# One row-half group per four token tiles in place of two, in a kernel of linear attention beside a gated feed-forward layer

## The chip, the cores and the metric

The kernel runs on one core of a Trainium2 chip. The metric is the device time of one execution in microseconds (us). The engines are PE (matrix products; its weight loads are listed as PEld), DVE (vector), ACT (scalar functions), POOL (a second vector-like engine) and SP, which here only issues transfers. They run side by side, each through its own queue in order, and wait for one another by semaphores.

## The reference

For 2048 tokens of 640 features the output is `g * a + (1 - g) * b`, with a gate `g = sigmoid(sum(x * gate_w))` per token. Branch `b` is a feed-forward layer:

```python
g = silu(x @ w_gate)          # 640 -> 1728
u = x @ w_up                  # 640 -> 1728
b = (g * u) @ w_down          # 1728 -> 640
```

Branch `a` is linear attention over 32 heads of 20 features:

```python
phi_q = concat(softmax(q @ w_phi), softmax(-(q @ w_phi)))   # 40 features per head
phi_k = concat(softmax(k @ w_phi), softmax(-(k @ w_phi)))
kv  = einsum("bhsf,bhsd->bhfd", phi_k, v)
num = einsum("bhqf,bhfd->bhqd", phi_q, kv)
a   = (num / (phi_q . sum(phi_k) + 1e-6)) @ wo
```

Two facts matter here. The hidden width 1728 is 13 x 128 + 64: the last chunk of the contraction in `(g * u) @ w_down` has only 64 rows. And the products with `w_down` and with `wo` go into the same sums, since the gate has been folded in before.

## The kernel before

The tokens are cut into 16 tiles of 128 (`NT`) and four blocks of four tiles (`NB`). The program is written out as a list of items in the string `ORDER`; each item is a letter with numbers, and the dictionary `ops` at the end maps the letter to a function. The items are emitted in this order, and every engine's queue gets its instructions in it. A tracker (`_Tracker`) adds the semaphore waits from the buffers that an instruction reads and writes. So `ORDER` alone sets which instruction stands behind which on each engine.

Up to the item N the list projects keys and values (U, V, K), builds the combined matrices (M, R), normalizes the keys (S on DVE, P on POOL) and sums `kv` (E). From there on the items are:

- `Q t` (`qtile`): the query projection of tile t on PE (ten matmuls of 320 columns), two exponentials on ACT into one of three `eq` buffers.
- `A t`, `B t`, `C t`: DVE's part of the normalization: a reduction (A), a product with the row `zb` (B), and a second reduction with five small instructions (C: `qw`, `qm`, `qd`, its reciprocal, `qc`).
- `c t` (`qmul`): POOL scales `eq` into `ph`, and SP transposes `ph` into `phiT` by a transfer.
- `F b.k` (`fitem`): chunk k of the hidden layer for block b. PE makes the gate and the up projection (five matmuls of 512 columns each) in the two banks of a PSUM pair, ACT a tanh into `hT` and a copy of the up part into one of three `us` buffers, DVE a product that reads the gate bank (line 332), POOL the product of both (line 328). `F b.13` is the last chunk, of 64 rows: it is laid out so that tiles 0 and 2 of a block lie in the rows 0 to 63 of `hT[.., 13, ..]` and tiles 1 and 3 in the rows 64 to 127, and `wd[:, 13, :]` holds the last 64 rows of `w_down` in both halves.
- `O b.part` (`oitem`): the attention output of block b in three parts, copied by ACT to `oT` and `ol`; `o b` (`omove`): SP moves `ol` into `oT` by four transfers.
- `W b.p` (`hitem`): the half-row products. For tiles 2p and 2p+1 of the block it takes a PSUM pair each and opens their sums with the 64-row chunk. The matmuls of the two tiles alternate, and since they use different halves of the rows of the array, two of them can run at once.
- `D b.u` (`ditem`): the output of tile u: 13 full chunks of `hT` and five of `oT`, each in two column parts of 320, so 36 matmuls, which go on with the sums that W opened; then ACT scales the sums by the gate (`omg`) into `osb` and SP stores them. The last tile (15) is done in three parts, of 320, 224 and 96 columns, so that the last store is small.
- `Z` transposes the denominators, from which `zb` is loaded; `J` (`gates`) makes the gate values on DVE and ACT; `L` loads the late weights.

PSUM has eight banks, used as four pairs. `next_pair` gives the pair that was used least recently and is not in `held`; W puts the pairs that it opens into `held` and D takes them out. An item that takes a pair waits for all that still reads it. `mm` emits a list of matmuls as one unit: the waits of all its operands stand ahead of its first matmul, and one semaphore is raised at its last. All matmuls have the line 300 (in `mm`), all activations the line 318.

The functions that the change touches are `hitem`, `ditem` and `parts`, the fills (`fills(3)`) and `ORDER`.

Of the kernel before, what the change touches and what calls it, by code (L numbers as in the profile page):

```python
# [1 line left out]

# [1 line left out]

# [4 lines left out]
P = 128  # L9
S_TOK = 2048  # L10
D = 640
# [3 lines left out]
NT = S_TOK // P  # L15
NB = 4
# [8 lines left out]
ACTF = mybir.ActivationFunctionType  # L25
# [3 lines left out]
BF16 = DT.bfloat16  # L29
# [12 lines left out]
U0.3 U1.3 U2.3 U0.4 U1.4 U2.4 V3 Y F0.1 M1 i3 M0 F0.0 M2 V4 M3 M4 K0 K1 I S0 V6 V5 S1 P0 K3 K2 P1 E0  # L42
V9 K4 E1 S3 V7 P3 K5 S2 V8 V10 S4 P2 P4 E2 R0 E3 K6 S5 P5 S6 i4 E4 V14 K7 K8 P6 V15 S7 R2 E5 K9 S8
P7 R1 E6 K10 S9 V12 P8 E7 P9 K11 S10 P10 F0.2 R3 F1.2 E8 E9 K12 E10 S11 S12 K14 S14 V11 K13 P11 P12
E11 K15 P14 R4 S13 P13 F1.9 S15 P15 E12 V13 T F1.8 E13 F1.11 E14 Q1 E15 Q0 Q2 N Z A1 A0 J A2 F0.7
F0.9 F1.4 B0 F1.12 B1 F0.4 L C0 F1.7 c0 F1.10 C1 F0.5 B2 c1 F0.11 Q3 C2 F1.0 F0.8 c2 F0.10 B3 Q4
F1.6 A3 C3 Q5 c3 F1.3 F0.13 F0.12 A4 F0.3 B4 F1.5 F0.6 O0.2 O0.1 O0.0 o0 C4 F1.1 F1.13 B5 A5 C5 Q6
c4 Q7 c5 Q8 W0.0 B7 A6 B6 C6 A7 c6 D0.1 D0.0 Q9 C7 W0.1 B8 A8 D0.2 C8 c7 Q10 D0.3 F2.10 F2.9 F2.2 c8
O1.2 A9 O1.1 B9 O1.0 B10 F2.8 o1 C9 Q11 c9 F2.5 F2.11 F2.4 Q12 B11 F2.3 A10 C10 B12 F2.7 A11 C11
W1.1 D1.3 D1.2 A12 c11 c10 Q14 W1.0 D1.0 A14 C12 D1.1 Q13 F3.2 F3.3 c12 O2.2 O2.1 B13 B14 O2.0 o2  # L50
F2.13 A13 F3.12 F3.5 F2.1 C14 Q15 F3.4 F3.9 F2.12 C13 F2.0 A15 c13 F2.6 c14 B15 F3.1 F3.0 F3.6 C15
c15 F3.13 W2.0 F3.7 D2.1 D2.0 F3.11 O3.2 O3.0 O3.1 F3.8 o3 F3.10 W2.1 D2.3 W3.0 D3.0 D3.1 D2.2 W3.1
D3.2 D3.3
"""


# [143 lines left out]
def _build(nc, A_x, A_wqkv, A_w_phi, A_wo, B_x, B_w_gate, B_w_up, B_w_down, gate_w, out):  # L200
    tr = _Tracker(nc)
    pe, act, dve, pool, sp = nc.tensor, nc.scalar, nc.vector, nc.gpsimd, nc.sync
# [3 lines left out]
    def sb(name, shape, dtype):  # L206
        t = nc.alloc_sbuf_tensor(name, list(shape), dtype)
        tr.reg(t, "sbuf", nc.lookup_mloc(t).addr)
        return t
# [5 lines left out]
    wd = sb("wd", [P, 14, D], BF16)  # L215
# [5 lines left out]
    osb = sb("osb", [P, 4, D], BF16)  # L221
# [10 lines left out]
    omg = sb("omg", [P, NT], F32)  # L232
# [9 lines left out]
    qd = sb("qd", [P, 2, 32], F32)  # L242
    qc = sb("qc", [P, 2, 66], F32)
    hT = sb("hT", [P, 2, 14, 512], BF16)

    wdbase = nc.lookup_mloc(wd).addr
    v1x = nc.alloc_sbuf_tensor_at("v1x", [P, NT - NV, 33 * 21], BF16, offset=wdbase)
# [32 lines left out]
    def bank(b, c0, c1, r0=0, r1=P):  # L280
        return ps[r0:r1, b * 512 + c0:b * 512 + c1]

    def halves(pr, n=320):

        return ps[:, pr * 1024:(pr + 1) * 1024].rearrange("p (b c) -> p b c", b=2)[:, :, 0:n]
# [5 lines left out]
    def mm(pairs):  # L291
        reads, writes = [], []
        for p in pairs:
            reads += [p[1], p[2]]
            writes.append(p[0])

        def fn():
            last = None
            for o, l, r, st, sp_, sk in pairs:
                last = pe.matmul(o, lhsT=l, rhs=r, start=st, stop=sp_, skip_group_check=sk)  # L300
            return last
        return run("pe", fn, list({id(a): a for a in reads}.values()), writes)

    def group(o, lr):
        n = len(lr)
        return [(o, l, r, i == 0, i == n - 1, False) for i, (l, r) in enumerate(lr)]
# [9 lines left out]
    def actop(o, i, func, scale=1.0):  # L316
        rd = [i] + ([scale] if isinstance(scale, bass.AP) else [])
        return run("act", lambda: act.activation(o, i, func, scale=scale), rd, [o])  # L318

    def copy(e, o, i):  # L320
        if e == "act":
            return actop(o, i, ACTF.Copy)
        eo = tr.eng[e]
        return run(e, lambda: eo.tensor_copy(o, i), [i], [o])
# [19 lines left out]
    def memset(e, a, v):  # L344
        eo = tr.eng[e]
        return run(e, lambda: eo.memset(a, v), [], [a])

    def dma(e, dst, src, transpose=False):
        eo = tr.eng[e]

        def fn():
            if transpose:
                return eo.dma_start_transpose(dst, src)
            return eo.dma_start(dst, src)  # L354
        rd = [src] if src.tensor.name in tr.base else []
        wr = [dst] if dst.tensor.name in tr.base else []
        return run(e, fn, rd, wr, dma=True)

    def select(ap, pattern, op, fill, base, cm):
        return run("pool", lambda: pool.affine_select(  # L360
            out=ap, in_=ap, pattern=pattern, compare_op=op, fill=fill, base=base,
            channel_multiplier=cm), [ap], [ap])
# [5 lines left out]
    out2 = out[0]  # L368
# [45 lines left out]
    def fills(i):  # L414
        if i < 2:
            v1v = (v1r, v1x)[i][:, :, :].rearrange("p b (h d) -> p b h d", d=DH + 1)
            memset("pool", v1v[:, :, H, :], 0.0)
            memset("pool", v1v[:, :, :, DH:DH + 1], 1.0)
        elif i == 2:
            memset("pool", ekr[:, :, 1280:FK], 0.0)  # L420
            memset("pool", krec[:, :, :], 0.0)
        elif i == 3:
            memset("pool", kvsb[:, :, :], 0.0)
            memset("pool", eq[:, :, 1280:FP], 0.0)
            memset("pool", qc[:, :, :], 0.0)
            memset("pool", hmask[:, :], 1.0)
            select(hmask[:, :], [[-40, 3]], ALU.is_ge, 0.0, 0, 1)
            select(hmask[:, :], [[40, 3]], ALU.is_gt, 0.0, 40, -1)
        else:
            memset("pool", ph[:, :, :], 0.0)  # L430
            memset("pool", zh[:, NCH:P], 0.0)

    for i in range(3):
        fills(i)
# [19 lines left out]
    held = set()  # L454

    def used(r):
        ring["lru"].remove(r)
        ring["lru"].append(r)
        return r

    def next_pair():
        return used([r for r in ring["lru"] if r < ring["n"] and r not in held][0])
# [268 lines left out]
    out_evs = []  # L731

    def stores_done():
        for n, v in out_evs[-4:-2]:
            sp.wait_ge(tr.sem[n], v)

    dpr = {}

    def parts(t):

        pr = dpr[t]
        if t < NT - 1:
            return [(2 * pr[0], 0, 320), (2 * pr[0] + 1, 320, D)]
        return [(2 * pr[0], 0, 320), (2 * pr[0] + 1, 320, 544), (2 * pr[1], 544, D)]

    def hitem(bt, p):

        todo = []
        for b in range(2):
            t = 4 * bt + 2 * p + b  # L750
            dpr[t] = [next_pair() for _ in range(1 + (t == NT - 1))]
            held.update(dpr[t])
            r = slice(64 * b, 64 * b + 64)
            todo.append([(bank(k, 0, c1 - c0), hT[r, bt % 2, 13, P * p:P * p + P], wd[r, 13, c0:c1], True, False, False)
                         for k, c0, c1 in parts(t)])
        mm([m for ab in zip_longest(*todo) for m in ab if m])

    def ditem(bt, u):
        buf = bt % 2
        t = 4 * bt + u  # L760
        tok = slice(P * u, P * u + P)
        ls = [(hT[:, buf, k, tok], wd[:, k, :]) for k in range(13)]
        ls += [(oT[:, buf, m, tok], wog[:, m, :]) for m in range(5)]
        n = len(ls)
        cols = [[(bank(k, 0, c1 - c0), l, r[:, c0:c1], False, i == n - 1, False) for i, (l, r) in enumerate(ls)]
                for k, c0, c1 in parts(t)]
        held.difference_update(used(r) for r in dpr[t])
        o = osb[:, t % 4, :]
        if t < NT - 1:
            mm([p for ab in zip(*cols) for p in ab])  # L770
            actop(o.rearrange("p (b c) -> p b c", b=2), halves(dpr[t][0]), ACTF.Copy, omg[:, t:t + 1])
            stores_done()
            out_evs.append(dma("sp", out2[t * P:(t + 1) * P, :], o))
            return
        for (b, c0, c1), e, ms in zip(parts(t), ("sp", "sp", "act"), cols):
            mm(ms)
            if e == "act":
                run("dve", lambda: dve.tensor_scalar(o[:, c0:c1], bank(b, 0, c1 - c0), omg[:, t:t + 1], None,  # L778
                                                     op0=ALU.mult, op1=ALU.bypass),
                    [bank(b, 0, c1 - c0), omg[:, t:t + 1]], [o[:, c0:c1]])  # L780
            else:
                actop(o[:, c0:c1], bank(b, 0, c1 - c0), ACTF.Copy, omg[:, t:t + 1])
            if e == "sp":
                stores_done()
            out_evs.append(dma(e, out2[t * P:(t + 1) * P, c0:c1], o[:, c0:c1]))
# [24 lines left out]
def bass_gated_mix__linear_kernel_hedgehog__swiglu_ffn__prompt_kernel(  # L810
    nc: bass.Bass,
    A_x: bass.AP,
    A_wqkv: bass.AP,
    A_w_phi: bass.AP,
    A_wo: bass.AP,
    B_x: bass.AP,
    B_w_gate: bass.AP,
    B_w_up: bass.AP,
    B_w_down: bass.AP,
    gate_w: bass.AP,  # L820
    out: bass.AP,
):
    _build(nc, A_x, A_wqkv, A_w_phi, A_wo, B_x, B_w_gate, B_w_up, B_w_down, gate_w, out)
# [28 lines left out]
```

## Time and profile before

| what | us |
|---|---|
| median of three runs | 287.82 (287.75 to 288.12) |
| the profiled execution, its own time | 289.13 |
| its span, first to last instruction | 287.8 |
| PE busy | 283.5 |
| DVE, ACT, POOL busy | 169.8, 152.9, 156.9 |
| first matmul of W0.0 and of W3.1, from the span's start | 131.6, 275.5 |

The granted clock of PE is 1.0 throughout. In the rows of a timeline the columns are the start, the duration, the engine, the line, the operation, what it writes and reads, the shape (with the rows and columns of the array in front, for a matmul), and how many instructions are merged into the row. In square brackets stands how long the engine had been idle, and what ended that. Matmuls are pipelined: a row's duration runs to the modelled end of its last one, and the next row starts before that, so what a matmul costs is read from the starts.

### The profile page before, as it was taken

Reading aid. Unit: us, or ns where it says so; the run is one execution under the profiler, and the core shown is the slowest. Engines: PE = TensorE matmul, PEld = TensorE weight load, DVE = VectorE, ACT = ScalarE, POOL = GpSimd, SP = SyncE. Lnnn points to the kernel's source line nnn. Section 1 sums busy time; section 2 is a strip of 40 time slices with the busy share of each in tenths; the row PEclk is TensorE's granted clock in tenths of the full one; section 3 lists DMA queues with packets and bytes.
Section 4 is the critical chain, followed back from the end, with each engine's and each line's share of the span. In section 5 each row is a group of like instructions: output and inputs, shape, how many; then the busy total and the mean of one; then the engine's idle time right before and its main releaser. Section 6 shows DMA issues by size and latency. Waiting matters only on the chain.

```text
span 287.8 us, 5041 instructions
## 1 busy us (share of the span) xinstructions
PE 283.5 (98%) x1999; PEld 173.5 (60%) x1999; DVE 169.8 (59%) x247; ACT 152.9 (53%) x264; POOL 156.9 (55%) x125
## 2 busy tenths in 40 slices
PE   7899999999999999999999999999999999999997
PEld 6567777675644555456675445767544457556766
DVE  2145757577479998769992787952566983010000
ACT  0668768766665557684434865132786543541112
POOL 8154899979635778947170757260465696130000
DMA  7985789000037264202243022051020053000101
GB/s 232 160 115 120 118 220 363 9 0 3 0 109 248 69 133 76 50 4 50 57 120 73 2 56 52 25 110 38 23 53 4 3 101 73 25 4 26 46 23 48
DMA packets 49374, 21.87 MB, mean 76 GB/s; under 512 B 39462, under 2 KB 49214, under 8 KB 49350
## 3 DMA queue, kind: packets, MB, share of 16 engines
q1 hardware_dynamic: 47830, 20.67, 31.5%
q10 hardware_dynamic: 1520, 0.87, 1.0%
q8 instruction: 16, 0.26, 0.4%
q14 instruction: 8, 0.07, 0.1%
HBM read 9.38 MB, written 2.62 MB: 42 GB/s over the span
## 4 chain that ended last, share of the span: by engine, by line
PE 96%; DMA 2%; ACTq 0%; DVE 0%; issue 0%
PE ps L300 96%; DMA xs<-in_A_x_dram 2%; ACTq L354 0%; PE ps L312 0%; DVE osb L778 0%
## 5 line engine op out<-in xcount | busy, mean ns | idle before, releaser
L328 POOL TENSOR_TENSOR hT<-hT,us 128x512 bf16<-128x512 bf16 (+1 forms) x56 | 66.2, 1193 | 68.4 <-ACT us L318 35.2
L332 DVE SCALAR_TENSOR_TENSOR hT<-hT,ps 128x512 bf16<-128x512 bf16 (+1 forms) x60 | 38.2, 648 | 50.8 <-ACT hT L318 45.0
L300 PE MATMUL ps<-xT,wg 128*128 128x512 bf16 x260 | 64.6, 379 | 0.0
L300 PE MATMUL ps<-xT,wu 128*128 128x512 bf16 x260 | 64.6, 379 | 0.0
L300 PE MATMUL ps<-wd,hT 128*128 128x320 bf16 (+3 forms) x462 | 62.6, 295 | 0.0
L300 PEld LDWEIGHTS ps<-wd,hT 128*128 128x128 bf16 (+1 forms) x462 | 41.8, 98 | 19.2 <-issue 3.1
L328 POOL TENSOR_TENSOR ph<-eq,qc 128x1320 bf16<-128x1320 bf16 x16 | 40.4, 2530 | 15.8 <-DVE qc L645 15.8
L300 PE MATMUL ps<-wqk,xT 128*128 128x320 bf16 x320 | 47.7, 299 | 0.0
L318 ACT ACTIVATE hT<-ps 128x512 bf16<-128x512 f32 (+1 forms) x60 | 34.0, 567 | 20.4 <-PE ps L300 15.2
L300 PEld LDWEIGHTS ps<-xT,wu 128*128 128x128 bf16 x260 | 25.5, 98 | 30.7
L318 ACT ACTIVATE us<-ps 128x512 bf16<-128x512 f32 (+1 forms) x60 | 34.1, 569 | 18.1 <-PE ps L300 17.2
L328 POOL TENSOR_TENSOR ekr<-ekr,krec 128x1280 bf16<-128x1280 bf16 x16 | 37.4, 2360 | 8.2 <-DVE krec L342 8.2
L300 PEld LDWEIGHTS ps<-xT,wg 128*128 128x128 bf16 x260 | 24.9, 98 | 27.7 <-ACT oT L318 1.2
L318 ACT ACTIVATE osb<-ps,omg 128x640 bf16<-128x640 f32 (+2 forms) x17 | 12.9, 758 | 53.0 <-PE ps L300 53.0
L300 PEld LDWEIGHTS ps<-wqk,xT 128*128 128x128 bf16 x320 | 30.6, 98 | 12.4
L318 ACT ACTIVATE eq<-ps 128x640 bf16<-128x640 f32 x32 | 22.5, 704 | 18.5 <-POOL ph L328 8.5
L339 DVE TENSOR_REDUCE ksum<-ekr 128x64 f32<-128x1280 bf16 x16 | 23.5, 1470 | 11.6 <-ACT ekr L318 11.6
L318 ACT ACTIVATE ekr<-ps 128x640 bf16<-128x640 f32 x32 | 22.3, 704 | 8.6 <-PE ps L300 8.1
L339 DVE TENSOR_REDUCE qz<-eq 128x64 f32<-128x1280 bf16 x16 | 23.6, 1478 | 3.6 <-ACT eq L318 3.6
L300 PE MATMUL ps<-wvg,xT 128*128 128x320 bf16 (+1 forms) x160 | 24.1, 300 | 1.2 <-DMA wvg<-in_A_wqkv_dram 1.1
L300 PE MATMUL ps<-wog,oT 128*128 128x320 bf16 (+2 forms) x165 | 24.7, 295 | 0.0
L339 DVE TENSOR_REDUCE qw<-ez 128x64 f32<-128x1280 bf16 x16 | 23.6, 1478 | 0.0
(73 smaller groups left out, 196.6 us busy)
## 6 DMA issues: line engine op xcount, KB each, us to landing
out_dram<-osb SPq DMA_DIRECT2D x15, 160.0 KB, 1.8
wd<-in_B_w_down_dram SPq DMA_DIRECT2D x1, 2080.0 KB, 10.4
wg<-in_B_w_gate_dram SPq DMA_DIRECT2D x1, 1040.0 KB, 10.0
wu<-in_B_w_up_dram SPq DMA_DIRECT2D x1, 1040.0 KB, 12.1
wg<-in_B_w_gate_dram SPq DMA_DIRECT2D x1, 800.0 KB, 6.1
wu<-in_B_w_up_dram SPq DMA_DIRECT2D x1, 800.0 KB, 7.6
wog<-in_A_wo_dram SPq DMA_DIRECT2D x2, 375.0 KB, 4.2
xs<-in_A_x_dram ACTq DMA_DIRECT2D x3, 160.0 KB, 3.9
```

The lines of the kernel that those rows point to most:

```text
L300: last = pe.matmul(o, lhsT=l, rhs=r, start=st, stop=sp_, skip_group_check=sk)
L318: return run("act", lambda: act.activation(o, i, func, scale=scale), rd, [o])
L328: return run(e, lambda: eo.tensor_tensor(o, a, b, op), [a, b], [o])
L332: return run("dve", lambda: dve.scalar_tensor_tensor(out=o, in0=a, scalar=s, in1=b, op0=op0, op1=op1), rd, [o])
L339: return run("dve", lambda: dve.tensor_reduce(o, i, AX.X, ALU.add), [i], [o])
```

## The change

W is now one item per block. It runs after D of the tiles 0 and 1 and before D of the tiles 2 and 3. D of tiles 0 and 1 opens their sums itself (`d_open`) and leaves them open; W closes these sums with its half-row products as last ones, opens those of tiles 2 and 3 with theirs as first ones, and then emits the output of tiles 0 and 1 (`d_out`). D of tiles 2 and 3 goes on with the sums and closes them. So a block has one group of eight half-row matmuls where it had two groups of four.

The third part of the last tile (96 columns) isn't in the group. It is a sum of its own, with a full-row matmul as its first: `hz` is a new 128 x 128 buffer whose rows 0 to 63 are zero (a POOL memset in `fills(3)`) and whose rows 64 to 127 are a DVE copy of that tile's half rows. The 36 matmuls of a D are emitted as two units, the 26 over `hT` and the ten over `oT`.

`ORDER` is new from N on. The items are the same but for W; their order differs, on all engines.

```diff
-E11 K15 P14 R4 S13 P13 F1.9 S15 P15 E12 V13 T F1.8 E13 F1.11 E14 Q1 E15 Q0 Q2 N Z A1 A0 J A2 F0.7
-F0.9 F1.4 B0 F1.12 B1 F0.4 L C0 F1.7 c0 F1.10 C1 F0.5 B2 c1 F0.11 Q3 C2 F1.0 F0.8 c2 F0.10 B3 Q4
-F1.6 A3 C3 Q5 c3 F1.3 F0.13 F0.12 A4 F0.3 B4 F1.5 F0.6 O0.2 O0.1 O0.0 o0 C4 F1.1 F1.13 B5 A5 C5 Q6
-c4 Q7 c5 Q8 W0.0 B7 A6 B6 C6 A7 c6 D0.1 D0.0 Q9 C7 W0.1 B8 A8 D0.2 C8 c7 Q10 D0.3 F2.10 F2.9 F2.2 c8
-O1.2 A9 O1.1 B9 O1.0 B10 F2.8 o1 C9 Q11 c9 F2.5 F2.11 F2.4 Q12 B11 F2.3 A10 C10 B12 F2.7 A11 C11
-W1.1 D1.3 D1.2 A12 c11 c10 Q14 W1.0 D1.0 A14 C12 D1.1 Q13 F3.2 F3.3 c12 O2.2 O2.1 B13 B14 O2.0 o2
-F2.13 A13 F3.12 F3.5 F2.1 C14 Q15 F3.4 F3.9 F2.12 C13 F2.0 A15 c13 F2.6 c14 B15 F3.1 F3.0 F3.6 C15
-c15 F3.13 W2.0 F3.7 D2.1 D2.0 F3.11 O3.2 O3.0 O3.1 F3.8 o3 F3.10 W2.1 D2.3 W3.0 D3.0 D3.1 D2.2 W3.1
-D3.2 D3.3
+E11 K15 P14 R4 S13 P13 F1.9 S15 P15 E12 V13 T F1.8 E13 F1.11 E14 Q1 E15 Q0 Q2 N A1 Z A0 A2 F1.3 F0.5
+F0.10 J B0 F0.11 C0 F0.12 L B1 B2 F1.1 c0 F0.3 F1.0 F1.10 C1 C2 c1 Q3 F1.7 F1.4 c2 F0.4 Q4 B3 F1.5
+A3 Q5 C3 c3 B4 F1.12 F1.6 F0.13 F0.9 B5 F0.6 F0.8 O0.2 A4 O0.0 C4 O0.1 F0.7 o0 Q6 c4 A5 C5 c5 A6 Q7
+F1.13 Q8 B6 D0.0 D0.1 C6 B7 W0 A7 c6 D0.3 Q9 C7 c7 A8 B8 D0.2 F2.6 A9 F2.3 B9 F2.7 F2.4 C9 O1.0 C8
+O1.2 O1.1 Q10 o1 F2.5 B10 c8 F2.2 c9 A10 Q11 C10 F2.12 A11 D1.1 D1.0 B11 c10 W1 D1.3 C11 Q12 B12
+D1.2 c11 F2.11 F3.0 Q13 Q14 B13 F3.11 F2.0 A12 F2.13 F2.10 A13 F2.9 F3.8 C12 F2.1 F3.2 c12 F3.7 O2.2
+C13 B14 O2.0 O2.1 o2 F3.1 A14 Q15 F3.9 A15 F2.8 B15 c13 F3.4 F3.3 C14 D2.0 C15 D2.1 W2 c14 c15 D2.3
+F3.10 F3.5 F3.6 O3.2 O3.0 O3.1 F3.12 o3 F3.13 D2.2 D3.1 D3.0 W3 D3.2 D3.3
...
+    hz = sb("hz", [P, P], BF16)
...
+            memset("pool", hz[:, :], 0.0)
...
     def parts(t):
 
-        pr = dpr[t]
-        if t < NT - 1:
-            return [(2 * pr[0], 0, 320), (2 * pr[0] + 1, 320, D)]
-        return [(2 * pr[0], 0, 320), (2 * pr[0] + 1, 320, 544), (2 * pr[1], 544, D)]
-
-    def hitem(bt, p):
-
-        todo = []
-        for b in range(2):
-            t = 4 * bt + 2 * p + b
-            dpr[t] = [next_pair() for _ in range(1 + (t == NT - 1))]
-            held.update(dpr[t])
-            r = slice(64 * b, 64 * b + 64)
-            todo.append([(bank(k, 0, c1 - c0), hT[r, bt % 2, 13, P * p:P * p + P], wd[r, 13, c0:c1], True, False, False)
-                         for k, c0, c1 in parts(t)])
-        mm([m for ab in zip_longest(*todo) for m in ab if m])
+        k = 2 * dpr[t]
+        return [(k, 0, 320), (k + 1, 320, D if t < NT - 1 else 544)]
+
+    def d_open(t):
+        dpr[t] = next_pair()
+        held.add(dpr[t])
+
+    def hitem(bt):
+
+
+        for p in range(2):
+            todo = []
+            for b in range(2):
+                t = 4 * bt + 2 * p + b
+                if p:
+                    d_open(t)
+                r = slice(64 * b, 64 * b + 64)
+                todo.append([(bank(k, 0, c1 - c0), hT[r, bt % 2, 13, P * p:P * p + P], wd[r, 13, c0:c1], p == 1, p == 0, False)
+                             for k, c0, c1 in parts(t)])
+            mm([m for ab in zip(*todo) for m in ab])
+        for t in (4 * bt, 4 * bt + 1):
+            held.remove(used(dpr[t]))
+            d_out(t)
+        if bt == NB - 1:
+            copy("dve", hz[64:P, :], hT[64:P, bt % 2, 13, P:2 * P])
+
+    def d_out(t):
+        o = osb[:, t % 4, :]
+        actop(o.rearrange("p (b c) -> p b c", b=2), halves(dpr[t]), ACTF.Copy, omg[:, t:t + 1])
+        stores_done()
+        out_evs.append(dma("sp", out2[t * P:(t + 1) * P, :], o))
 
     def ditem(bt, u):
...
-        cols = [[(bank(k, 0, c1 - c0), l, r[:, c0:c1], False, i == n - 1, False) for i, (l, r) in enumerate(ls)]
-                for k, c0, c1 in parts(t)]
-        held.difference_update(used(r) for r in dpr[t])
+        if u < 2:
+            d_open(t)
+        cols = [[(bank(k, 0, c1 - c0), l, r[:, c0:c1], u < 2 and i == 0, u > 1 and i == n - 1, False)
+                 for i, (l, r) in enumerate(ls)] for k, c0, c1 in parts(t)]
+        if t < NT - 1:
+            both = [p for ab in zip(*cols) for p in ab]
+            mm(both[:26])
+            mm(both[26:])
+            if u > 1:
+                held.remove(used(dpr[t]))
+                d_out(t)
+            return
         o = osb[:, t % 4, :]
-        if t < NT - 1:
-            mm([p for ab in zip(*cols) for p in ab])
-            actop(o.rearrange("p (b c) -> p b c", b=2), halves(dpr[t][0]), ACTF.Copy, omg[:, t:t + 1])
-            stores_done()
-            out_evs.append(dma("sp", out2[t * P:(t + 1) * P, :], o))
-            return
-        for (b, c0, c1), e, ms in zip(parts(t), ("sp", "sp", "act"), cols):
+        held.remove(used(dpr[t]))
+        ps3 = parts(t) + [(2 * next_pair(), 544, D)]
+        cols.append(group(bank(ps3[2][0], 0, D - 544), [(l, r[:, 544:D]) for l, r in [(hz[:, :], wd[:, 13, :])] + ls]))
+        for (b, c0, c1), e, ms in zip(ps3, ("sp", "sp", "act"), cols):
             mm(ms)
```

More of the change, by code (lines that the diff above doesn't have):

```diff
@@ L1 @@
 from __future__ import annotations
-from itertools import zip_longest
 import concourse.bass as bass
```

## The prediction

> **What bounds the kernel now.** I read the page's busy times and chain first, then the timeline of PE around a row-half group, then the timelines of DVE, POOL and ACT where the new order puts them closest to PE.
>
> ```profile
> span 287.8 us, 5041 instructions
> PE 283.5 (98%) x1999; PEld 173.5 (60%) x1999; DVE 169.8 (59%) x247; ACT 152.9 (53%) x264; POOL 156.9 (55%) x125
> PE   7899999999999999999999999999999999999997
> ...
> PE ps L300 96%; DMA xs<-in_A_x_dram 2%; ACTq L354 0%; PE ps L312 0%; DVE osb L778 0%
> ```
>
> PE is busy 98% of the span and 96% of the chain that ended last is its own line 300. From 9.6 us to the end the chain never leaves PE. So matmul time taken away is time gained, and any wait put on PE is time lost; nothing else counts.
>
> The next rows are PE's alone: a group of four half-row matmuls (W) ahead of a product (D), a D without W, and a W ahead of an F.
>
> ```profile
> 131.61 0.31 PE L300 MATMUL ps<-wd,hT 64*128 64x320 bf16 x2
> 131.61 0.45 PE L300 MATMUL ps<-wd,hT 64*128 64x320 bf16 x4
> 131.38 0.30 PE L300 MATMUL ps<-wqk,xT 128*128 128x320 bf16 x1
> 131.61 4.08 PE L300 MATMUL ps<-wd,hT 64*128 64x320 bf16 x30
> 135.53 1.52 PE L300 MATMUL ps<-wog,oT 128*128 128x320 bf16 x10
> 136.89 3.69 PE L300 MATMUL ps<-wd,hT 128*128 128x320 bf16 x26
> 140.42 1.52 PE L300 MATMUL ps<-wog,oT 128*128 128x320 bf16 x10
> 234.68 0.45 PE L300 MATMUL ps<-wd,hT 64*128 64x320 bf16 x4
> 235.06 0.60 PE L300 MATMUL ps<-xT,wg 128*128 128x512 bf16 x2
> ```
>
> Read starts, not durations, since matmuls overlap. 26 full matmuls take 136.89 to 140.42, so 0.136 us each. The last Q matmul starts at 131.38, the first half-row one at 131.61: 0.23 us, which is 0.095 over the cadence. Two half-row matmuls start together (x2 is done at 0.31, x4 at 0.45), so one pair costs about 0.145. From the first half-row matmul to the next full one it is 0.38 (234.68 to 235.06): two pairs at 0.145 would be 0.29, so leaving costs some 0.09 as well.
>
> **The change, part by part.**
>
> *Eight groups become four.* One group of four costs 0.095 + 0.38 = 0.475 us; eight, 3.80. The rows from 131.61 to 140.42 agree: 3.92 for a D with W, 3.53 without, 0.39 between them. A group of eight adds two more pairs: 0.475 + 2 x 0.145 = 0.765; four, 3.06. The number of half-row matmuls stays at 32 but for the last tile's third one, of 96 columns. That one becomes a full-row matmul over hz, at the cadence of the last part (13 matmuls from 284.98 to 285.53, 0.04 each); the last pair of the last group is 224 wide on one side and gives 0.04 back. Sum: 3.06 - 3.80 = **-0.74 us**. If the third and fourth pair of a group run at the plain cadence of 0.136 it is -0.81; if they were to pay as much as the leaving does, 0.09 for each, -0.02. I take -0.74, since 0.145 is the row of the same instruction.
>
> [...]
>
> *hz.* Its memset on POOL is one of the size of ident's (205 ns) and stands in a row of others at 17 to 18 us, ahead of a POOL idle of 5.46 us before the first kmul: nothing. Its DVE copy (the nearest, of 128x128 from PSUM, is 0.35 us) comes when DVE idles 30.6 us before its last instruction, and is needed two D later: nothing. Without that cover 0.35.
>
> *D opens its banks, W closes two and opens two.* Before W0 the banks of tiles 2 and 3 were last used by F1.13 and Q8; two D of 4.9 us lie between. Nothing. D's wait for oT now stands before its last ten matmuls alone, 3.5 us later than its start. The outputs of the first two tiles come together after W; ACT's two copies (0.79 each) run beside the next D, and the SP stores (0.33 to issue, 1.8 to land) put c6's transpose some 1.6 us behind W0, with D0.3, Q9, D0.2 and four F before O1 needs it: nothing.
>
> *Three pairs instead of four around O3.* New: W2 opens tile 10, and D2.2 stands only after F3.10 F3.5 F3.6 O3.2 O3.0 O3.1 F3.12 F3.13. All these share three PSUM pairs; so O3.1 takes the pair of F3.6, and F3.12 that of O3.2. The rows of O3 in the trace, with PE and ACT:
>
> ```profile
> 249.26 1.39 PE L300 MATMUL ps<-phiT,kvsb 120*64 120x512 bf16 x12
> 249.37 0.60 ACT L318 ACTIVATE us<-ps 128x512 bf16<-128x512 f32 x1 [0.48 <-PE ps L300]
> 249.86 0.59 ACT L318 ACTIVATE oT<-ps 128x512 bf16<-128x512 f32 x1
> ```
>
> O starts at 249.26; its third part is two thirds in, some 0.8 us later (250.05). The copy of the F before it ends at 249.97. With a semaphore and a weight load (0.1) between, O3.1 is 0.08 us late. O3.2's own copy ends at 250.45, the next F starts at 250.58: enough. Cost **+0.08**, between 0 and 0.3 (both waits bite).
>
> *The order of the other engines.* Up to N it is the same but for A1 and Z. From Z to O0 both tables hold 18 F (2.16 us), F0.13 (1.10) and three Q (1.36), so O0 would start at 122.86 again. J (0.9 us with its trip to ACT) now stands right before B0, which waits for zb until 86.5 anyway: at most 0.3. F0.7, the last h of block 0, comes after O0, where F1.1 was (POOL product done at 129.1); A4 (1.40) is now ahead of it on DVE, whose idle of 1.06 takes most of that: done about 129.5, D0.0 starts at 126.35 + three Q + F1.13 = 131.5. Two us to spare. F2.8 has two F (4.3 us) before D2.0, and an F's product is done 2.0 us after its last matmul (F3.10: 255.0 to 257.0): 2.3 less up to 1 of DVE's queue.
>
> The one place without room is C1 and C2, now back to back ahead of F1.7's product on DVE (L332). Here is one C beside POOL's work, and POOL:
>
> ```profile
> 94.22 1.48 DVE L339 TENSOR_REDUCE qw<-ez 128x64 f32<-128x1280 bf16 x1
> 95.73 1.47 DVE L332 SCALAR_TENSOR_TENSOR qw<-qz,qw 128x64 f32<-128x64 f32 x1
> 97.24 1.08 DVE L640 TENSOR_TENSOR qm<-qw,qz 128x64 f32<-128x64 f32 x1
> ...
> 99.17 0.68 DVE L332 SCALAR_TENSOR_TENSOR hT<-hT,ps 128x512 bf16<-128x512 bf16 x1
> ```
> ```profile
> 94.69 2.43 POOL L328 TENSOR_TENSOR ph<-eq,qc 128x1320 bf16<-128x1320 bf16 x1
> 97.08 1.16 POOL L328 TENSOR_TENSOR hT<-hT,us 128x512 bf16<-128x512 bf16 x1
> ```
>
> The two small instructions end just after the POOL instruction they began beside: this C takes 4.95 us (94.22 to 99.17), the next 4.93, C3 3.67 (one wait, 111.53 to 115.20), C4 2.9 (no POOL beside it). Now the walk. F1.10 stands in the slot that ends at 98.18; its tanh is done at 97.90, its product on DVE starts then, and C1 0.6 later, at 98.53. F1.7's product starts two C later: 104.3 (both free) to 108.4 (both at 4.95). It frees the PSUM pair that F1.5 takes, whose slot starts at 107.37 (98.18 + Q3, three F, Q4); with 0.69 for the product and a weight load it must start by 106.55. C2 can meet only c1 on POOL, as F1.7's POOL product waits behind it: 3.67 as C3. C1 meets a backlog of F products: 3.67 to 4.95. So 105.9 to 107.2, with the limit in its middle. I take **0**, and keep 0 to 1.9 us. What follows is tied to it: after F1.7's product come two more (1.9 with it), B3 (up to 1.8), F1.5's (0.65), A3 (1.40) and C3 (3.67), so C3 ends 9.4 us later; c3 on POOL (2.4 to 2.9) and its transpose (3.6 to land) then reach O0 at 121.3 to 123.1 against 122.86.
>
> [...]
>
> **The sum.** -0.74 + 0.08 + 0 = -0.66 us. The profiled execution took 289.13 for a span of 287.8; the runs shown have a median of 287.82 and differ by 0.37. The saving is in the span, so I take it from the median: 287.82 - 0.66 = 287.16.
>
> **Rivals.**
> - *DVE holds PE between 107 and 123 us, a little.* For it: the limit lies in the middle of my estimate. Against: DVE waits shorten themselves, for POOL runs out of products when DVE is late. F1.7's product at 106.7 to 107.8 costs 0.15 to 1.25: 287.3 to 288.4, within 0.2% (0.58 us, about what a measurement of this kernel can tell from no change).
> - *The same, in full: slower.* From 107.85 on F1.5 waits 1.3 us, more than is gained plus 0.58; C1 and C2 must then take 9.3 of the 9.9 us that two fully held ones take. 4.95 and 4.93 in a row in the trace speak for it, C3's 3.67 against it. 288.4 to 289.1, and F0.6 (the pair of F1.12, whose product is behind C3 and B4) could add up to 0.5.
> - *The groups save nothing,* the third and fourth pair paying 0.09 each and the three pairs 0.3: 288.0. The 0.145 between pairs speaks against it.
>
> **How the numbers follow.** My forecast, no wait over 0.1 us: 0.50. Some wait, 0.1 to 1.3 us: 0.24. Full: 0.20. Groups that save little: 0.06. Faster by over 0.2% is the first: 0.50; same 0.30; slower 0.20. The likeliest alone lies between 287.0 (-0.81, no wait) and 287.25. The range reaches down to 286.9 and up through the second rival into the first half of the third, 288.7.
>
> **What will show it.** Four rows of eight half-row matmuls, each some 0.67 us from its first to the next full one; D with 26 and 10 matmuls at 0.136. PE starting O0 at 122.86 shows that the order holds; a gap before F1.5's first matmul, with F1.7's product (L332) as its releaser, shows the first rival, and one before O0 the landing of c3. Before O3.1 a gap of 0.1. I am wrong if PE waits anywhere else after 9.6 us: before D0.0 or D2.0 (F0.7, F2.8 late), or in a group, where the second tile pair's banks are not yet free.

## The result, and the profile after

| | kernel before | changed kernel |
|---|---|---|
| median of 22 runs each, us | 287.85 (287.39 to 288.93) | 287.40 (286.91 to 287.88) |
| ratio | | 0.9984, 95% interval 0.9976 to 0.9992 |
| profiled execution: span, own time | 287.8, 289.13 | 286.5, 287.78 |

The changed kernel is faster by 0.16%, 0.45 us (0.23 to 0.69 by the interval). That is less than the 0.2% that the prediction set as its bound, and less than the 0.66 us that it forecast, which lies just inside the interval. The spans of the two profiled executions differ by 1.3 us, three times as much, and the first thing to learn here is why.

The page of the changed kernel, its span and busy times, and its chain by engine:

```profile
span 286.5 us, 5033 instructions
PE 283.6 (99%) x1999; PEld 174.9 (61%) x1999; DVE 170.3 (59%) x248; ACT 152.6 (53%) x264; POOL 155.6 (54%) x126
...
PE 99%; DVE 0%; issue 0%
```

PE is still the bound, and has as many matmuls. The chain in order of time (start, length, what) shows the only place between the start and the end where it leaves PE:

```profile
8.80 69.19 PE ps L298 x640
77.99 0.05 PE ps L310
78.04 28.62 PE ps L298 x140
106.66 0.14 issue
106.80 177.82 PE ps L298 x1154
```

Up to the transpose of Z both orders are the same, but for A1, a reduction on DVE that now stands ahead of it. Here is the row of the transpose, first of the kernel before, then of the changed one:

```profile
78.70 0.22 PE L312 MATMUL ps<-ident,zh 120*128 120x120 bf16 x1
```
```profile
77.83 0.22 PE L310 MATMUL ps<-ident,zh 120*128 120x120 bf16 x1
```

So 0.87 of the 1.30 us had been won before the first place where the new order could tell on PE. It isn't the change's: in the profile before, PE stood 1.1 us near its start waiting for a piece of `wvg` to be loaded, and in this one it didn't. What the change did is in the time from Z's transpose to the start of PE's last matmul: 207.01 us before (78.70 to 285.70), 206.58 after (77.83 to 284.40). That is **0.43 us less**, which agrees with the 0.45 of the medians: what is left of a median beside this length is 80.84 us before and 80.82 after. This length is the ruler of what follows. It repeats to 0.01 us where a kernel was run twice, while the times of one kernel scatter by over 1.5 us (those of the kernel before, in the table).

Three places make up the 0.43. The first is the group of eight, in PE's rows:

```profile
135.83 3.69 PE L298 MATMUL ps<-wd,hT 128*128 128x320 bf16 x26
139.36 1.52 PE L298 MATMUL ps<-wog,oT 128*128 128x320 bf16 x10
140.81 4.36 PE L298 MATMUL ps<-wd,hT 64*128 64x320 bf16 x34
145.01 1.52 PE L298 MATMUL ps<-wog,oT 128*128 128x320 bf16 x10
```

From 140.81 to 145.01 are 4.20 us for 8 + 26 matmuls, and from 135.83 to 139.36 are 3.53 for 26: 0.67 for the eight, and 0.095 for going in. By the starts of the single matmuls the first pair of a group takes 0.146, the second and third 0.136, and the last pair with the way out 0.231; the first full matmul behind a group takes 0.146, not 0.136. So a group of four costs 0.484 and one of eight 0.756: eight of the one, 3.87, become four of the other, 3.02. That is 0.85 less, and the matmul over hz takes 0.04 of it back, so the change saves 0.81 us here.

The second place is the gap at 106.66. DVE there:

```profile
97.06 0.69 DVE L330 SCALAR_TENSOR_TENSOR hT<-hT,ps 128x512 bf16<-128x512 bf16 x1 [1.47 <-ACT hT L316]
97.66 1.48 DVE L337 TENSOR_REDUCE qw<-ez 128x64 f32<-128x1280 bf16 x1
99.17 1.05 DVE L330 SCALAR_TENSOR_TENSOR qw<-qz,qw 128x64 f32<-128x64 f32 x1
100.26 1.08 DVE L639 TENSOR_TENSOR qm<-qw,qz 128x64 f32<-128x64 f32 x1
...
102.19 1.48 DVE L337 TENSOR_REDUCE qw<-ez 128x64 f32<-128x1280 bf16 x1
103.70 1.15 DVE L330 SCALAR_TENSOR_TENSOR qw<-qz,qw 128x64 f32<-128x64 f32 x1
...
105.97 1.88 DVE L330 SCALAR_TENSOR_TENSOR hT<-hT,ps 128x512 bf16<-128x512 bf16 x3
```

and POOL and PE beside it:

```profile
97.88 3.37 POOL L326 TENSOR_TENSOR hT<-hT,us 128x512 bf16<-128x512 bf16 x3
102.35 2.42 POOL L326 TENSOR_TENSOR ph<-eq,qc 128x1320 bf16<-128x1320 bf16 x1 [1.10 <-DVE qc L644]
```
```profile
105.14 1.52 PE L298 MATMUL ps<-wqk,xT 128*128 128x320 bf16 x10
106.80 1.24 PE L298 MATMUL ps<-xT,wg 128*128 128x512 bf16 x5
```

C1 runs from 97.66 to 102.19, C2 to 105.97: 4.53 and 3.78 us, where `qw` and `qm` take up to 1.15 beside POOL's work and 0.23 alone. Both are long in C1, and they end 0.09 us after an F product on POOL (100.14 and 101.25); in C2 it is `qw` alone, and it ends 0.08 us after c1 (104.78). F1.7's product (105.97) frees the PSUM pair of F1.5. Ten Q matmuls at 0.136 from 105.14 would put F1.5 at 106.50; it starts at 106.80, **0.30 us late**.

The third, smaller place is O3. The matmul before it to the first one behind it is 1.71 us apart, in the three other blocks and in the kernel before 1.63. Of the 0.09, 0.06 is lost where the third part, O3.1, begins (0.27 from the matmul before, where it is 0.21 elsewhere) and the rest before its last matmul (0.029, where it is 0.003 to 0.005 elsewhere). -0.81 + 0.30 + 0.09 = -0.42, and the ruler shows -0.43.

### The profile page after: what moved, and what is told of

Read it like the earlier page. It is cut to its first block, busy times and chain, and to the rows that moved or that the text cites. A ratio compares the mean times of both kernels' runs of the same rounds, so it can differ in the third digit from the quotient of the medians.

```text
span 286.5 us, 5033 instructions
## 1 busy us (share of the span) xinstructions
PE 283.6 (99%) x1999; PEld 174.9 (61%) x1999; DVE 170.3 (59%) x248; ACT 152.6 (53%) x264; POOL 155.6 (54%) x126
## 4 chain that ended last, share of the span: by engine, by line
PE 99%; DVE 0%; issue 0%
PE ps L298 97%; PE ps L484 1%; PE ps L310 1%; DVE osb L798 0%
## 5 line engine op out<-in xcount | busy, mean ns | idle before, releaser
L326 POOL TENSOR_TENSOR hT<-hT,us 128x512 bf16<-128x512 bf16 (+1 forms) x56 | 65.4, 1176 | 78.5 <-ACT us L316 43.3
L326 POOL TENSOR_TENSOR ph<-eq,qc 128x1320 bf16<-128x1320 bf16 x16 | 39.8, 2488 | 14.6 <-DVE qc L644 14.6
L298 PE MATMUL ps<-wvg,xT 128*128 128x320 bf16 (+1 forms) x160 | 24.7, 306 | 0.0
```

Source lines behind the costliest of these rows:

```text
L326: return run(e, lambda: eo.tensor_tensor(o, a, b, op), [a, b], [o])
```

## The experiments

The theory to be tested: the groups save 0.8 us by switching less often, F1.5 gives back 0.30 because DVE does C1 and C2 ahead of F1.7's product, beside POOL's products, and O3 gives back 0.09 because three PSUM pairs turn there. In the edits below, a line of `ORDER` is given only as far as it changes.

### C2 behind F1.7

```diff
-F0.3 F1.0 F1.10 C1 C2 c1 Q3 F1.7 F1.4 c2
+F0.3 F1.0 F1.10 C1 c1 Q3 F1.7 C2 F1.4 c2
```

> The changed kernel with C2 moved behind F1.7 in the order, so that DVE makes F1.7's product before C2. Theory (the groups save 0.78 us, F1.5 waits 0.30 for F1.7's product behind C1 and C2, O3 costs 0.09): no gap before F1.5's first matmul, the time from Z's transpose to PE's last matmul falls from 206.58 to 206.28, and the time to about 287.1, 0.25% under the kernel before. Rival (PE would meet the same wait later, at O0 for c3's transpose or at F0.6 for its pair, so the gap only moves): 206.5 or more, time as the changed kernel's, 287.4.

Measured: 206.28 us on the ruler, no gap before F1.5:

```profile
105.26 1.52 PE L298 MATMUL ps<-wqk,xT 128*128 128x320 bf16 x10
106.62 1.24 PE L298 MATMUL ps<-xT,wg 128*128 128x512 bf16 x5
```

The wait came from C2's place and didn't come back later. The time was 287.56 us (ratio 0.9989, 0.9978 to 1.0), though, 0.16 above that of the changed kernel as first measured, where 0.3 below was expected. The ruler and the median contradict each other here; the repetition below shows which of them speaks of the kernel.

### c0 early

```diff
-L B1 B2 F1.1 c0 F0.3
+L B1 B2 c0 F1.1 F0.3
```

> The changed kernel with c0 moved ahead of F1.1, so that POOL does it 2 us earlier and three F products are no longer queued on POOL when C1 runs on DVE; the order on DVE stays. If DVE's small two-input instructions wait for POOL instructions (theory), C1 takes 2.9 to 3.7 us in place of 4.5, F1.7's product starts at most 105.2 in place of 105.97, and the gap before F1.5 (0.30) is gone: 206.28 from Z to the last matmul, 287.1. If C1 is long for another reason (rival), the gap stays at 0.3 and the time at 287.4.

Measured: 206.28 us on the ruler, 286.89 us (ratio 0.9968, 0.9957 to 0.9979), and no gap before F1.5:

```profile
104.40 1.52 PE L298 MATMUL ps<-wqk,xT 128*128 128x320 bf16 x10
105.76 1.24 PE L298 MATMUL ps<-xT,wg 128*128 128x512 bf16 x5
```

DVE's order was left as it is; only POOL's work is at another time. DVE, then POOL:

```profile
96.92 1.48 DVE L337 TENSOR_REDUCE qw<-ez 128x64 f32<-128x1280 bf16 x1
98.44 0.23 DVE L330 SCALAR_TENSOR_TENSOR qw<-qz,qw 128x64 f32<-128x64 f32 x1
98.70 1.07 DVE L639 TENSOR_TENSOR qm<-qw,qz 128x64 f32<-128x64 f32 x1
...
100.62 1.48 DVE L337 TENSOR_REDUCE qw<-ez 128x64 f32<-128x1280 bf16 x1
```
```profile
92.25 3.00 POOL L326 TENSOR_TENSOR ph<-eq,qc 128x1320 bf16<-128x1320 bf16 x1
95.21 4.48 POOL L326 TENSOR_TENSOR hT<-hT,us 128x512 bf16<-128x512 bf16 x4
```

`qw` begins 0.14 us before the third of the four F products on POOL ends (98.58) and takes 0.23, not 1.05; `qm` falls beside the fourth (98.55 to 99.69) and still takes 1.07. C1 takes 3.70, not 4.53. So C1 is long because of what POOL does beside it: the same instructions, in the same order, with the same data, 0.83 us faster. The same holds over all 16 tiles: in each of the ten profiles 9 to 13 of the 32 `qw` and `qm` products take over 0.3 us, every one of them ends 0.08 to 0.09 us after a POOL instruction, and all the others take 0.22 to 0.24.

### The new order with two groups of four

```diff
-D0.0 D0.1 C6 B7 W0 A7 c6 D0.3
+W0.0 D0.0 D0.1 C6 B7 W0.1 A7 c6 D0.3
```

and so on in the other blocks, with the functions of the kernel before.

> The new order alone: two groups of four row-half matmuls per block as in the kernel before, everything else in the order of the changed kernel. Theory: the order itself costs 0.39 us (0.30 at F1.5, 0.09 at O3), so 207.4 from Z to the last matmul against 207.01 before, and 288.2. Rival (the order, not the groups, is what gains): 206.6 and 287.4.

Measured: 209.14 us and 290.14 us (ratio 1.0078, 1.0065 to 1.0091). The two losses are there (0.30 at F1.5, 0.09 at O3), and a third that I had not expected, of 1.76 us:

```profile
132.67 4.08 PE L299 MATMUL ps<-wd,hT 64*128 64x320 bf16 x30 [1.69 <-ACT eq L317]
```

W0.0 opens two pairs at once, and the second is Q7's, whose exponentials end on ACT only then, at 132.53; in the changed kernel D0.1 opens it 4.9 us after D0.0 has begun. ACT:

```profile
131.09 1.44 ACT L317 ACTIVATE eq<-ps 128x640 bf16<-128x640 f32 x2 [2.44 <-DVE qw L331]
```

0.30 + 0.09 + 1.76 = 2.15 over the 207.01 before is 209.16. So the rival, that the order gains by itself, is out: alone it loses, and without the third wait it would still lose some 0.4. And at W0 the new order needs the new way of opening sums.

### The old order with one group

```diff
-W0.0 B7 A6 B6 C6 A7 c6 D0.1 D0.0 Q9 C7 W0.1 B8 A8 D0.2 C8 c7 Q10 D0.3
+B7 A6 B6 C6 A7 c6 D0.1 D0.0 W0 D0.2 Q9 C7 B8 A8 C8 c7 Q10 D0.3
...
-W2.0 F3.7 D2.1 D2.0 F3.11 O3.2 O3.0 O3.1 F3.8 o3 F3.10 W2.1 D2.3 W3.0 D3.0 D3.1 D2.2 W3.1
+F3.7 D2.1 F3.11 O3.2 O3.0 O3.1 F3.8 o3 F3.10 D2.0 W2 D2.3 D2.2 D3.0 D3.1 W3
```

> The one group per block in the order of the kernel before, changed only around the D items, so that W stands between two D and two D. Theory: no gap before the F after Q4, groups of 0.74 us each, 0.09 at O3 as three pairs are left there too: 206.3 from Z to the last matmul, 0.7 less than before, and 287.15. Rival (the groups save less than the rows say): 206.6 or more and 287.4 or more.

Measured: 206.96 us and 287.86 us (ratio 0.9999, 0.9989 to 1.0008), where the rival's figures lie. But there is no gap before the F after Q4, and the groups are as cheap as in the changed kernel (0.650 us from the first half-row matmul to the next full one in both); the gain is eaten by one wait that this edit made itself:

```profile
243.80 1.38 PE L299 MATMUL ps<-phiT,kvsb 120*64 120x512 bf16 x12 [0.70 <-DMA phiT<-ph]
```

O3 lost the cover of D2.0, which I had moved behind it, and stands 0.77 us for c15's transpose. 207.01 - 0.81 + 0.77 = 206.97. As a test of the group alone it is spoiled in its total; read by places it agrees.

### The groups cut in two

After the first four half-row matmuls, before the others:

```diff
+            if p == 0:
+                t = 4 * bt + 3
+                d_open(t)
+                mm([(bank(k, 0, c1 - c0), hT[:, bt % 2, 0, 3 * P:4 * P], wd[:, 0, c0:c1], True, False, False)
+                    for k, c0, c1 in parts(t)])
```

> The changed kernel with each group of eight cut in two by two full matmuls: the first two of tile 3's D (its two column parts over chunk 0) stand between the four half-row matmuls that close tiles 0 and 1 and the four that open tile 2 and go on with tile 3. No matmul more or less, and no other item moved. Theory (the price is that of switching in and out, 0.2 us a time): four switches in and four out more, 0.81 us, so 207.39 from Z's transpose to PE's last matmul against 206.58, and 288.2. Rival (what a group costs is in its pairs, not in its ends): 206.6 to 206.8, and 287.5.

Measured: 207.41 us and 288.34 us (ratio 1.0024, 1.001 to 1.0038). This is the switch by itself: same matmuls, same order of everything else, each group only interrupted.

```profile
140.60 4.57 PE L298 MATMUL ps<-wd,hT 64*128 64x320 bf16 x34
145.01 1.52 PE L298 MATMUL ps<-wog,oT 128*128 128x320 bf16 x10
```

4.41 us for the 34 matmuls that took 4.20: 0.21 for going out and in once, 0.84 for the four blocks. This is what the groups saved (0.85 by the rows, before the 0.04 of hz), and it is undone without touching the order.

### W2 closes three tiles

With c0 early as above, and in block 2

```diff
-C14 D2.0 C15 D2.1 W2 c14 c15 D2.3 F3.10 F3.5 F3.6 O3.2 O3.0 O3.1 F3.12 o3 F3.13 D2.2 D3.1 D3.0 W3
+C14 D2.0 C15 D2.1 c14 c15 D2.2 W2 D2.3 F3.10 F3.5 O3.2 O3.0 O3.1 F3.6 o3 F3.12 F3.13 D3.1 D3.0 W3
...
-            mm(both[:26])
+            mm(both[:24])
+            mm(both[24:26])
```

Not shown is the part of the edit by which W closes the sums that it finds open and opens the others.

> c0 early as in the run of that name, and in block 2 D2.2 ahead of W2, so that W2 closes three tiles and opens one and no PSUM pair is held while O3 runs; F3.6 behind O3; c14 and c15 ahead of D2.2; the 26 matmuls of a D in two units of 24 and 2, so that D3.1 can start before F3.12's product is there. Theory (O3.1 waits 0.09 us for the pair of the F before it, since only three pairs turn): the O3 block takes 1.63 us from the matmul before it to the one after it, not 1.71, and 206.2 from Z to the last matmul; 286.8 to 287.1. Rival (O3 was late for oT or for phiT): 1.71 stays, 206.28.

Measured: 206.19 us on the ruler, 287.14 us (ratio 0.9971, 0.9958 to 0.9984), the time just above the 286.8 to 287.1 expected. O3 takes 1.63 us as elsewhere:

```profile
256.90 1.38 PE L298 MATMUL ps<-phiT,kvsb 120*64 120x512 bf16 x12
258.22 1.04 PE L298 MATMUL ps<-xT,wg 128*128 128x512 bf16 x4
```

In the changed kernel the same two starts are further apart:

```profile
254.49 1.47 PE L298 MATMUL ps<-phiT,kvsb 120*64 120x512 bf16 x12
255.89 0.82 PE L298 MATMUL ps<-xT,wg 128*128 128x512 bf16 x3
```

So the loss at O3 goes with the pair held there. The edit moves other things too (D2.2, F3.6, the transposes), so it doesn't single out the pair of the F before; ACT's copy out of that pair runs from 254.60 to 255.20 in the changed kernel, O3.1's weight load starts at 255.31 and its first matmul at 255.34, where 255.28 was due; that fits the theory and doesn't show it. A late `phiT` is out: O3.2, the first part, reads all four tiles of it too and begins on time, 0.31 us after the matmul before, as in the other blocks.

From Z on no PE wait is left in this kernel; its chain is one piece to the last matmul:

```profile
78.02 206.20 PE ps L298 x1294
```

With both waits gone the whole 0.81 shows: 207.01 - 0.81 = 206.20, and the ruler has 206.19. In time it can't be told from the kernel with c0 early alone (286.89, and 287.18 in the repetition below): 0.09 us is less than these medians scatter.

### The first two once more

> The kernel with C2 behind F1.7 once more. It and the one with c0 early had the same 206.28 us from Z to the last matmul, but medians of 287.56 and 286.89. If the difference is in the loads at the start, which vary from one execution to the next, both come out within 0.3 of each other here, at 286.9 to 287.4. If it belongs to the kernel, it is 287.5 again.

Measured: 206.28 us, 286.98 us (ratio 0.9976, 0.9964 to 0.9988).

> The kernel with c0 early once more, beside the one with C2 late. Loads at the start: within 0.3 us of that one, 286.9 to 287.4. A property of the kernel: 286.9 again, 0.6 below it.

Measured: 206.28 us, 287.18 us (ratio 0.9975, 0.9965 to 0.9984). The order of the two has turned round: 0.67 us apart the first time, 0.20 the other way now. So what set them apart was not in the kernels. In the profiles of these four runs Z's transpose starts at 77.94 and 77.25 (C2 late), 77.09 and 77.53 (c0 early), on code that is the same up to there, and everything behind it takes 206.28. Taken together, C2 late has 287.26 and c0 early 287.07, each with twice the runs; both beat the kernel before, as the ruler, 0.73 us shorter for them, says they should.

## Why the prediction was right and wrong

- *PE sets the end, nothing else counts.* Right: the differences in the ruler are found again as PE's own, place by place, to 0.02 us.
- *Eight groups become four, -0.74 us.* Right in mechanism, a little small: 0.81. I had given the two pairs that a group gains the 0.145 of the first; they run at the plain 0.136, the case that I had put at -0.81. That this case gives the 0.81 to the hundredth is luck, since two small terms cancel. The first full matmul behind a group costs 0.01 more, which I had left out (four groups fewer save 0.04). And hz's matmul costs 0.04, which I had balanced against the last pair of 320 beside 224 columns: that pair gave back 0.004 (0.646 us from the last group's first matmul to the next full one, 0.650 in the others), since it takes as long as its wider half. The way in was 0.095 as read. Going out and in costs 0.21 us together, by the groups cut in two. No run shows what PE does in that time.
- *hz, the outputs behind W, the wait for oT: nothing.* Right: no gap in PE at any of them (hz's own matmul is counted above). The memset took 0.22 us on POOL, the copy 0.19 on DVE, both in idle time. (The 0.35 that I had for a copy of 128x128 is the mean over copies of three widths; those of 128x128 took 0.22.)
- *Three pairs around O3, +0.08.* Right in size: 0.09, in O3.1. The loss goes with the pair held there; that O3.1 waits for the copy out of the F before is argued from the times.
- *C1 and C2 ahead of F1.7's product: 0.* This is the term that was mis-sized: it measured **0.30**. The walk itself held. I had F1.7's product at 105.9 to 107.2 with the limit at 106.55; it came at 105.97, which is 106.84 on the scale of the profile before (0.87 later at Z), 0.29 past the limit. C2 was 3.78 for the 3.67 I took, C1 4.53 within its 3.67 to 4.95. The failed step is the choice: with the estimate centred on the limit I wrote 0, but a wait can't be negative, so half of that range costs nothing and the other half costs up to 0.65. The mean of it, if all of the range is as likely, is some 0.16, and the sum would have been -0.5.
- *c3's transpose at O0, F0.7 before D0.0, F2.8 before D2.0.* Right: no gap. C3 ended 9.2 us after F1.7's product began, for the 9.4 worked out.
- *The median.* -0.66 forecast, -0.45 measured. My first rival, a little wait at F1.5, is what happened (I had it cost 0.15 to 1.25), so the gain of over 0.2% that I thought likeliest (0.50, against 0.24 for this rival) became one below that bound.
- *The sum against the profiled execution.* I took the saving from the median, and that was right: the profiled execution before was 1.3 us above it by its loads. Compared span with span the change would seem to bring 1.3 us.

## What to carry to other kernels

Where one engine is full, cost a new order by walking each of its waits to the instruction that frees it, and where the walk ends on its limit, put the mean of the wait into the sum and not the zero: a wait has only one sign. Matmuls that use part of the rows are best kept in one run, since here going out and in cost 0.21 us, more than a pair itself at 0.136. And compare two profiles from an item behind the loads to the end, not by their spans; differences of a quarter per cent then show in single executions, where medians of a dozen runs can still turn round.

## What was not expected of the hardware

The first full matmul behind a half-row group took 0.01 us longer than the next of its kind in every profile (0.146 for 0.136 at 320 columns), and so did the first pair within a group (but for W0.0 in the new order with two groups, which PE began after standing still: 0.135). A 128x64 fp32 instruction of DVE with two inputs in SBUF, of 0.22 us alone, took up to 2.35 us beside POOL in the changed kernel, while the products that read one input from PSUM never took over 0.69. The start of the program, up to Z's transpose, took 77.1 to 78.7 us in ten profiles of kernels that differ there at most by one memset and the place of one reduction on DVE; in the slowest PE stood 1.1 us for a piece of `wvg`, in the next (78.27) 0.7 us for one of `xs`.
